# A tail reordered, its last product split, and each pair of row chunks stored by one transfer

## The chip, the cores and the metric

One core of a Trainium2 chip runs the kernel. The time is the device time of one execution in microseconds (us). The kernel before takes 466.84 us (median of 3 runs, 465.91 to 466.93). Kernels are compared only within the same rounds. Spans come from one profiled execution; its time is some 1.8 us longer than its span (before: 468.84 us for a span of 467.1).

Engines in the profile: PE is the matmul engine and PEld its weight loads, DVE is VectorE, ACT ScalarE, POOL GpSimd, SP SyncE. "SPq" is SyncE's sequencer while it issues a transfer. A transfer has landed when the last increment of its semaphore has come. A bank is a PSUM tile of 128x512 float32.

## The reference, cut to what matters

Two layers: attention with an exponential feature map, then a mix of the 64 lowest frequencies, a channel product and a rectifier.

```python
x = attention(q, k, v, w_phi)            # (8, 576, 512)
X = np.fft.rfft(x, axis=1)               # 64 modes are kept
Yr = Xr @ w_r - Xi @ w_i                 # one 512x512 product per mode
Yi = Xr @ w_i + Xi @ w_r
y = np.fft.irfft(Y, n=576, axis=1)
u = x + y
return u + np.maximum(u @ w_ch, 0.0)     # (8, 576, 512) float32, 9.44 MB
```

## The kernel before

The 64 modes are worked in eight "octets". The mode weights stream from DRAM until shortly before the end; the octet that needs the last of them is the last one. What this case is about comes after it: turn the last octet's sum (`yst`) and its product with `w_ch` (`zst`) back into rows, add them to the rows kept so far, rectify, and store 9.44 MB.

The rows of one pair of batches (`bp`) are cut into nine chunks of 128 rows. A row of a batch is `9 * p + c`, with `p` from 0 to 63. Chunk `n < 8` belongs to batch `n // 4`; on its partition `64 * a + p` it holds row `9 * p + 4 * a + n % 4`. Chunk 8 holds row `9 * p + 8` of both batches.

```python
pst_cm = tc.tile_pool(name="pst", bufs=8, space=bass.MemoryType.PSUM)   # eight single banks
...
    def back(p, c, bp, table, src, r, stop=True):          # frequencies back to rows
        if c < 8:
            pe.matmul(p, lhsT=table[r, c % 4, :], rhs=src[r, 2 * bp + c // 4, :], ...)
...
    class Absorb:           # octets 0 to 5 of one chunk, added into the kept rows
        def sums(self): ...                                # 3 matmuls into two banks
        def keep_x(self): ...                              # DVE: x += p
        def keep_w(self): ...                              # ACT: xw = q
...
    while mixq:             # one weight block after another
        mix(*key, wts.pop(key), XTb[g % 2], bank)
        ...
        if g == NG - 1 and i == 1:
            yst = pb.tile([128, DMODEL], BF16, name="yst")
            dve.tensor_tensor(out=yst, in0=py, in1=yacc[:, o, :], op=ALU.add)
            put(yst, o, yall, (0, 2))
            ...                                            # 4 transposes into pt
            act.copy(yT, pt)
            ...                                            # product: 4 matmuls of 512 columns
            act.copy(zst, pz)
            put(zst, o, zall, (1, 3))
...
    class Last:             # octets 6 and 7 and the store, two chunks at a time
        def base(self, which): ...                         # kept rows, by an identity
        def late(self, which): ...                         # octets 6, 7 from yl
        def straight(self, which): ...                     # octet 7 from yst, zst (first chunks)
        def relu(self): ...                                # ACT: rl = relu(q)
        def store(self):
            ...
            dve.tensor_tensor(out=o, in0=self.pp, in1=self.rl, op=ALU.add)   # 128x1024
            i, c = n // 4, n % 4
            for a in range(2):
                (sp, pool)[a].dma_start(
                    rows[i][:, 4 * a + c:4 * a + c + 2, :], o[64 * a:64 * a + 64])
```

A pair of chunks is thus stored by two transfers, one from SyncE and one from GpSimd. Each takes 64 partitions to 64 places of 4096 bytes.

Of the kernel before, what the change touches and what calls it, by code (L numbers as in the profile page):

```python
# [10 lines left out]
F32 = mybir.dt.float32  # L11
# [32 lines left out]
def kernel(  # L44
# [495 lines left out]
    pin_cm.__exit__(None, None, None)  # L540
    ps1_cm.__exit__(None, None, None)
    ps2_cm.__exit__(None, None, None)
    pst_cm = tc.tile_pool(name="pst", bufs=8, space=bass.MemoryType.PSUM)
    pst = pst_cm.__enter__()

    def bank(shape=(128, DMODEL), dt=F32):
        return pst.tile(list(shape), dt, name="pt", tag="pt")

    pb_cm = tc.tile_pool(name="pb", bufs=2)
    pb = pb_cm.__enter__()  # L550
# [3 lines left out]
    yl = pw.tile([128, B_, DMODEL], BF16, name="yl", tag="wt")  # L554
    CI = pb.tile([128, 5, 128], BF16, name="CI", bufs=1)
    CL = pb.tile([128, 5, 128], BF16, name="CL", bufs=1)
    CM = pb.tile([128, 4, 128], BF16, name="CM", bufs=1)


    def inverse_tables():  # L560
# [22 lines left out]
        def calc(in0, s1, s2, op0=ALU.mult, op1=ALU.add):  # L583
            f = small[:, used[1]:used[1] + 1]
            used[1] += 1
            dve.tensor_scalar(out=f, in0=in0, scalar1=s1, scalar2=s2, op0=op0, op1=op1)
            return f
# [4 lines left out]
        late = calc(calc(bits(pi, 4, 1), 8.0, 48.0), 1.0, jt)  # L592
        jm, tm, rm, b0 = bits(pi, 5, 3), bits(pi, 4, 1), bits(pi, 3, 1), bits(pi, 0, 7)
        last = calc(calc(tm, 4.0, jm), 1.0, 56.0)
        b0 = calc(b0, 0.0, 1.0, ALU.is_equal, ALU.mult)
        for dst, m, r, only in ((CI, mode, r, None), (CL, late, r, None), (CM, last, rm, b0)):
            n = 512 if only is not None else 640
            ph = calc(r, -S_ / 4.0, S_ / 4.0)
            amp = calc(r, -4.0 / S_, 2.0 / S_)
            if m is mode:  # L600
                half = calc(calc(m, 0.0, -0.5, ALU.is_equal, ALU.mult), 1.0, 1.0)
                amp = calc(amp, half, 0.0)
            if only is not None:
                amp = calc(amp, only, 0.0)
            dve.tensor_scalar(out=ang[:, :n], in0=tok[:, :n], scalar1=m, scalar2=ph,
                              op0=ALU.mult, op1=ALU.add)
            dve.tensor_scalar(out=rnd[:, :n], in0=ang[:, :n], scalar1=1.0 / S_, scalar2=MAGIC,
                              op0=ALU.mult, op1=ALU.add)
            dve.tensor_scalar(out=rnd[:, :n], in0=rnd[:, :n], scalar1=-MAGIC,
                              scalar2=-float(S_), op0=ALU.add, op1=ALU.mult)  # L610
            dve.tensor_tensor(out=ang[:, :n], in0=ang[:, :n], in1=rnd[:, :n], op=ALU.add)
            act.activation(rnd[:, :n], ang[:, :n], ACT.Sin, scale=2.0 * math.pi / S_)
            dve.tensor_scalar_mul(out=dst.rearrange("p c s -> p (c s)"), in0=rnd[:, :n],
                                  scalar1=amp)
# [31 lines left out]
    class Absorb:  # L646
# [3 lines left out]

        def sums(self):
            r = slice(0, 96)
            self.p, self.q = bank(), bank()
            back(self.p, self.n, self.bp, CI, yall, r)
            pe.matmul(self.q, lhsT=ident_b, rhs=xw[:, self.bp, self.n, :],
                      start=True, stop=False)
            back(self.q, self.n, self.bp, CI, zall, r)
# [25 lines left out]

        todo.append(both)
    ab = [Absorb(*c) for c in chunks]
    todo += [c.all for c in ab[:-3]]

    def fill(n):
        for _ in range(n):
            if todo:  # L690
                todo.pop(0)()

    def put(src, o, dst, copies):
        if o < 6:
            sp.dma_start(dst[16 * o:16 * o + 16], src)
        else:
            for s in copies:
                r = 32 * s + 16 * (o - 6)
                sp.dma_start(yl[r:r + 16], src)

    todo = [inverse_tables] + todo
    while mixq:
        key = mixq.pop(0)
        g, o, i = key[0], key[1] // 2, key[1] % 2
        if key not in wts:
            next_w(1)
        mix(*key, wts.pop(key), XTb[g % 2], bank)
        next_w(1)
        left = len(mixq)
        n = -(-max(len(todo) - 33, 0) // (left - 7)) if left > 7 else -(-len(todo) // max(left, 1))  # L710
        if g == NG - 1 and i == 1:
            py = pys.pop(o)
            yst = pb.tile([128, DMODEL], BF16, name="yst")
            dve.tensor_tensor(out=yst, in0=py, in1=yacc[:, o, :], op=ALU.add)
            put(yst, o, yall, (0, 2))
            end = left == 0
            if end:
                ab[-3].sums()
                ab[-3].keep_x()
            fill(min(n, 1))  # L720
            pt = bank([128, 4, 128], BF16)
            for dc in range(4):
                pe.transpose(pt[:, dc, :], yst[:, dc * 128:(dc + 1) * 128], ident_b)
            yT = pb.tile([128, 4, 128], BF16, name="yT")
            act.copy(yT, pt)
            if end:
                ab[-2].sums()
                ab[-2].keep_x()
                ab[-3].keep_w()
            fill(min(n - 1, 1))  # L730
            pz = bank()
            for dc in range(4):
                pe.matmul(
                    pz, lhsT=yT[:, dc, :], rhs=wchb[:, dc, :],
                    start=(dc == 0), stop=(dc == 3))
            zst = pb.tile([128, DMODEL], BF16, name="zst")
            act.copy(zst, pz)
            put(zst, o, zall, (1, 3))
            if end:
                ab[-2].keep_w()  # L740
                ab[-1].all()
            fill(max(n - 2, 0))
        else:
            fill(n)
    assert not todo
    pst_cm.__exit__(None, None, None)
    pst1 = ctx.enter_context(tc.tile_pool(name="pst1", bufs=4, space=bass.MemoryType.PSUM))
    pst2 = ctx.enter_context(tc.tile_pool(name="pst2", bufs=2, space=bass.MemoryType.PSUM))

    class Last:  # L750

        def __init__(self, bp, ns):
            self.bp, self.ns = bp, ns
            self.early = bp == 0 and ns[0] < 4

        def base(self, which):
            if which:
                self.q = [pst1.tile([128, DMODEL], F32, name="qq", tag="qq") for _ in self.ns]
            else:
                self.pp = pst2.tile([128, 2, DMODEL], F32, name="pp", tag="pp")  # L760
                self.p = [self.pp[:, a] for a in range(len(self.ns))]
            for a, n in enumerate(self.ns):
                if which:
                    pe.matmul(self.q[a], lhsT=ident_b, rhs=xw[:, self.bp, n, :],
                              start=True, stop=False)
                else:
                    pe.matmul(self.p[a].rearrange("p (g e) -> p g e", g=4), lhsT=ident_b,
                              rhs=chunk(self.bp, n), start=True, stop=False)
# [7 lines left out]
        def straight(self, which):  # L776
            if self.early:
                for a, n in enumerate(self.ns):
                    pe.matmul((self.q if which else self.p)[a], lhsT=CM[:, n],
                              rhs=(yst, zst)[which], start=False, stop=True)  # L780

        def relu(self):
            self.rl = pb.tile([128, 2, DMODEL], F32, name="rl")
# [1 line left out]
                act.activation(self.rl[:, a], self.q[a], ACT.Relu)  # L785

        def store(self):
            bp, n = self.bp, self.ns[0]
            rows = [out[2 * bp + i].rearrange("(p c) e -> p c e", c=9) for i in range(2)]
            if n == 8:  # L790
                o = pw.tile([128, DMODEL], F32, name="ofr", tag="wt")
                dve.tensor_tensor(out=o, in0=self.pp[:, 0], in1=self.rl[:, 0], op=ALU.add)
                for i in range(2):
                    (sp, pool)[i].dma_start(rows[i][:, 8, :], o[64 * i:64 * i + 64, :])
                return
            o = pw.tile([128, 2, DMODEL], F32, name="of", tag="wt")
            dve.tensor_tensor(out=o, in0=self.pp, in1=self.rl, op=ALU.add)
            i, c = n // 4, n % 4
            for a in range(2):
                (sp, pool)[a].dma_start(  # L800
                    rows[i][:, 4 * a + c:4 * a + c + 2, :], o[64 * a:64 * a + 64])

    seq = [Last(bp, ns) for bp in range(NP) for ns in ((0, 1), (2, 3), (4, 5), (6, 7), (8,))]
    seq[0].base(1)
    seq[0].late(1)
    seq[0].straight(1)
    seq[0].relu()
    for g, s in enumerate(seq):
        t = seq[g + 1] if g + 1 < len(seq) else None
        if t:  # L810
            t.base(1)
        s.base(0)
        if t:
            t.late(1)
        s.late(0)
        s.straight(0)
        if t:
            t.straight(1)
            t.relu()
        s.store()  # L820
# [31 lines left out]
```

## Time and profile before

| | before |
|---|---|
| time, median | 466.84 us |
| span of the profiled run | 467.1 us |
| last weights used by the last octet | 422.94 us |
| first store issued | 432.79 us |
| last addition ends | 458.2 us |
| DMA share while storing | 0.93 to 0.98 |

The first view is the table of busy time by stretch. Its columns are the stretch, its length, the busy time and instruction count of PE, PEld, DVE, ACT and POOL, the granted clock, the mean busy share of the 16 DMA engines, and the GB/s that they moved.

```profile
428.00:434.00 6.00, 5.74 (x31) 2.10 (x31) 1.53 (x2) 3.29 (x7) 0.55 (x1) 1.00 0.20 48
434.00:440.00 6.00, 6.00 (x37) 1.74 (x34) 4.98 (x5) 3.99 (x8) 2.12 (x4) 1.00 0.93 274
440.00:452.00 12.00, 12.00 (x72) 3.67 (x68) 10.26 (x10) 8.70 (x17) 4.75 (x9) 1.00 0.95 309
452.00:464.00 12.00, 5.03 (x30) 1.46 (x30) 5.50 (x5) 3.97 (x8) 3.19 (x6) 0.79 0.98 323
464.00:467.00 3.00, 0.00 (x0) 0.00 (x0) 0.00 (x0) 0.00 (x0) 0.00 (x0) 0.50 0.27 78
```

From 428 to 434 us the DMA engines are nearly idle. After that they are busy nearly all the time, at 274 and then at about 310 GB/s, and from 452 us on the compute engines run out of work first. The head of the tail therefore decides when the stores can start, and the stores decide how long it then takes.

The timeline of the head, in order of start (start, duration, engine, operation, output and inputs; in brackets the engine's idle time before it and what ended it):

```profile
422.94 0.67 PE L37 MATMUL pt<-wt,XT 128*32 128x512 bf16 x8 [1.67 <-DMA wt<-in_moe_w_i_dram]
...
423.65 0.69 DVE L37 TENSOR_TENSOR yst<-pt,yacc 128x512 bf16<-128x512 f32 x1 [2.09 <-PE pt L37]
...
424.89 0.58 ACT L37 COPY yT<-pt 128x512 bf16<-128x512 bf16 x1 [2.95 <-PE pt L37]
...
425.53 1.04 PE L37 MATMUL pt<-wchb,yT 128*128 128x512 bf16 x4
...
426.65 0.58 ACT L37 CAST zst<-pt 128x512 bf16<-128x512 f32 x1 [0.68 <-ACT xw L37]
...
431.53 1.23 DVE L37 TENSOR_TENSOR of<-pp,rl 128x1024 f32<-128x1024 f32 x1 [3.90 <-PE pp L37]
...
432.79 2.66 SPq L37 DMA_DIRECT2D out_dram<-of  x2
```

From the last octet's matmuls to the first store there are 9.85 us, nearly all of it serial.

### The profile page before, as it was taken

How to read it: one execution, taken by the hardware profiler on the slowest of the kernel's cores; microseconds unless marked ns; L12 is line 12 of the kernel's file. 1: busy time of each engine (PE TensorE's matmuls, PEld its weight loads, DVE VectorE, ACT ScalarE, POOL GpSimd, SP SyncE). 2: the span in 40 equal slices, each digit the busy share in tenths (PEclk: the TensorE clock that was granted, in tenths of full speed). 3: DMA queues.
4: the chain of work that ended last, by engine and by line, in shares of the span. 5: the costliest groups of instructions: out<-in, count | busy, mean ns of one | idle time of the engine just before them, and what ended most of it. 6: DMA issues, size and time to landing. Idle time of an engine off the chain costs nothing.

```text
span 467.1 us, 9757 instructions
## 1 busy us (share of the span) xinstructions
PE 337.8 (72%) x4084; PEld 207.5 (44%) x4084; DVE 269.1 (58%) x488; ACT 281.1 (60%) x475; POOL 92.7 (20%) x130
## 2 busy tenths in 40 slices
PE   0377677758788777788768778129997656997991
PEld 0246465636565555466546546005443322332330
DVE  5275877564666566777675676563331113773882
ACT  2566988766787786688777765123443323664771
POOL 5130322104112121122210112203221110000331
PEclk9998999888888798799997989659998997999996
DMA  8999999999999999999999999999999999992797
GB/s 193 207 177 220 226 210 228 229 229 136 225 208 229 229 213 222 229 209 227 229 229 207 229 207 208 207 207 207 207 214 214 216 216 211 207 177 50 241 317 254
DMA packets 86301, 99.27 MB, mean 213 GB/s; under 512 B 2800, under 2 KB 79728, under 8 KB 86256
## 3 DMA queue, kind: packets, MB, share of 16 engines
q0 software_dynamic: 77264, 81.80, 102.9%
q1 hardware_dynamic: 8992, 16.85, 11.8%
q8 instruction: 32, 0.52, 0.4%
q14 instruction: 13, 0.11, 0.1%
HBM read 163.64 MB, written 9.44 MB: 371 GB/s over the span
## 4 chain that ended last, share of the span: by engine, by line
issue 37%; DMA 21%; PE 16%; ACT 8%; POOL 8%; DVE 7%; POOLq 0%; ACTq 0%
PE pt L37 8%; DMA wt<-in_moe_w_r_dram 8%; DMA wt<-in_moe_w_i_dram 6%; DMA kb<-in_k_dram 5%; PE one L37 4%; POOL wt L37 4%; PE two L37 4%; DVE m L37 4%; ACT AQ L37 3%; DMA qb<-in_q_dram 3%; POOL out_dram L37 2%; ACT AB L37 2%; DVE zall L37 2%; ACT qT L37 1%; ACT kT L37 1%
## 5 line engine op out<-in xcount | busy, mean ns | idle before, releaser
L37 ACT CAST xw<-pt 128x512 bf16<-128x512 f32 x72 | 42.0, 586 | 59.5 <-PE pt L37 58.3
L37 ACT ACTIVATE AB<-two 128x1024 bf16<-128x1024 f32 x64 | 62.8, 1051 | 7.5 <-DVE mk L37 5.1
L37 ACT ACTIVATE AQ<-two 128x1024 bf16<-128x1024 f32 x64 | 63.1, 1055 | 2.8 <-PE two L37 2.6
L37 PE MATMUL pt<-wchb,xT 128*128 128x512 bf16 x144 | 38.6, 393 | 19.3 <-DVE xT L37 19.3
L37 DVE TENSOR_REDUCE m<-two 128x8 f32<-128x1024 f32 x32 | 39.2, 1224 | 19.4 <-PE two L37 19.3
L37 DVE TENSOR_REDUCE mk<-two 128x8 f32<-128x1024 f32 x32 | 38.9, 1219 | 19.5 <-PE two L37 19.0
L37 POOL DMA_DIRECT2D wt<-in_moe_w_i_dram x30 | 26.5, 882 | 110.1 <-PE one L37 63.8
L37 POOL DMA_DIRECT2D wt<-in_moe_w_r_dram x29 | 25.6, 881 | 95.7 <-PE one L37 62.0
L37 DVE TENSOR_TENSOR va<-vn,ee 128x1152 bf16<-128x1152 f32 x32 | 42.0, 1356 | 0.0
L37 DVE RECIPROCAL rd<-one 128x6 f32<-128x6 f32 x48 | 9.4, 196 | 50.3 <-PE one L37 50.3
L37 ACT COPY kT<-one 128x512 bf16<-128x512 bf16 (+1 forms) x32 | 19.2, 640 | 30.0 <-PE one L37 30.0
L37 PEld LDWEIGHTS <-minus 96*128 96x128 bf16 x288 | 27.4, 114 | 20.1 <-issue 14.8
L37 DVE TENSOR_TENSOR xs<-pt,xs 128x512 bf16<-128x512 f32 x36 | 24.3, 691 | 18.9 <-PE pt L37 18.5
L37 PE MATMUL two<-qT,w2blk 128*128 128x512 bf16 x64 | 29.9, 467 | 6.3 <-ACT AQ L37 6.3
L37 PEld LDWEIGHTS <-XT 128*32 128x32 bf16 x512 | 18.0, 179 | 35.9 <-issue 22.9
L37 PE MATMUL two<-w2blk,qT 128*128 128x256 bf16 x128 | 21.2, 292 | 16.5 <-ACT AB L37 11.9
L37 DVE COPY xT<-pt 128x512 bf16<-128x512 bf16 x36 | 15.1, 422 | 27.9 <-PE pt L37 27.9
L37 PEld LDWEIGHTS <-xs 128*128 128x128 bf16 x304 | 24.1, 98 | 14.9 <-issue 7.6
L37 PE MATMUL two<-mT,minus 96*128 96x128 bf16 x256 | 30.3, 252 | 0.0
L37 PE MATMUL pt<-wt,XT 128*32 128x512 bf16 x208 | 18.6, 434 | 13.6 <-DMA wt<-in_moe_w_i_dram 9.9
L37 PEld LDWEIGHTS <-qT 128*128 128x128 bf16 x144 | 14.4, 103 | 31.3 <-issue 28.4
L37 DVE TENSOR_TENSOR xs<-one,rd 128x384 bf16<-128x384 f32 x48 | 26.8, 558 | 1.6
(113 smaller groups left out, 679.3 us busy)
## 6 DMA issues: line engine op xcount, KB each, us to landing
wt<-in_moe_w_i_dram POOLq DMA_DIRECT2D x30, 1024.0 KB, 23.7
wt<-in_moe_w_r_dram POOLq DMA_DIRECT2D x29, 1024.0 KB, 23.9
vn<-in_v_dram SPq DMA_DIRECT2D x16, 576.0 KB, 7.8
kb<-in_k_dram POOLq DMA_DIRECT2D x16, 288.0 KB, 17.6
qb<-in_q_dram POOLq DMA_DIRECT2D x16, 288.0 KB, 17.7
out_dram<-of SPq DMA_DIRECT2D x16, 256.0 KB, 5.8
out_dram<-of POOLq DMA_DIRECT2D x16, 256.0 KB, 5.3
yacc<-in_moe_w_r_dram POOLq DMA_DIRECT2D x1, 1024.0 KB, 12.5
```

The costliest lines, as they stand in the source:

```text
L37: ins = f(*args, **kwargs)
```

## The change

Its intent is to start the stores earlier and to issue fewer of them. The first two chunks are handled one by one and in PSUM banks of their own; all that doesn't depend on the last octet is summed before it. The last product runs in halves of 256 columns, with ACT and DVE each copying one half. All 36 chunks are absorbed before the last octet (before: 33). And every pair is stored by one transfer of 128 partitions, by SyncE and GpSimd in turn. The ninth chunk, in before two stores of 64 rows, becomes one store of 128 rows from SyncE, with 128 in front on its DRAM side; that is not in the cut.

```diff
-    pst_cm = tc.tile_pool(name="pst", bufs=8, space=bass.MemoryType.PSUM)
+    pst = ctx.enter_context(tc.tile_pool(name="pst", bufs=4, space=bass.MemoryType.PSUM))
+    pst2 = ctx.enter_context(tc.tile_pool(name="pst2", bufs=2, space=bass.MemoryType.PSUM))
...
-    todo += [c.all for c in ab[:-3]]
+    todo += [c.all for c in ab]
...
+        if not mixq:                                  # just ahead of the last octet
+            for l in seq[:2]:
+                for which in (1, 0):
+                    l.base(which)
+                    l.late(which)
         mix(*key, wts.pop(key), XTb[g % 2], bank)
...
+            for h in range(2):                        # yst, yT, product and zst in halves
+                dve.tensor_tensor(out=yst[:, H * h:H * h + H], ...)
...
+            act.copy(zst[:, 0:H], pz[0])
+            dve.tensor_copy(zst[:, H:], pz[1])
...
         def store(self):
-            i, c = n // 4, n % 4
-            for a in range(2):
-                (sp, pool)[a].dma_start(
-                    rows[i][:, 4 * a + c:4 * a + c + 2, :], o[64 * a:64 * a + 64])
+            eng = (sp, pool)[n // 2 % 2]
+            rows = out[2 * bp + n // 4]
+            eng.dma_start(
+                bass.AP(tensor=rows.tensor, offset=rows.offset + n % 4 * DMODEL,
+                        ap=[[4 * DMODEL, 2], [9 * DMODEL, 64], [1, w * DMODEL]]),
+                o.rearrange("p a e -> p (a e)") if w > 1 else o)
...
-    seq = [Last(bp, ns) for bp in range(NP) for ns in ((0, 1), (2, 3), (4, 5), (6, 7), (8,))]
+    seq[0:1] = [Last(0, (0,)), Last(0, (1,))]
```

The partitions are `64 * a + p`, so the DRAM side of one transfer has to count `a` (2) first, then `p` (64), then the row.

More of the change, by code (lines that the diff above doesn't have):

```diff
@@ L542, with banks @@
     ps2_cm.__exit__(None, None, None)
-    pst_cm = tc.tile_pool(name="pst", bufs=8, space=bass.MemoryType.PSUM)
-    pst = pst_cm.__enter__()
+    pst = ctx.enter_context(tc.tile_pool(name="pst", bufs=4, space=bass.MemoryType.PSUM))
+    pst2 = ctx.enter_context(tc.tile_pool(name="pst2", bufs=2, space=bass.MemoryType.PSUM))
     def bank(shape=(128, DMODEL), dt=F32):
         return pst.tile(list(shape), dt, name="pt", tag="pt")
+    def banks(dt=F32):
+        return pst2.tile([128, 2, DMODEL * (1 if dt == F32 else 2)], dt, name="pp", tag="pp")
     pb_cm = tc.tile_pool(name="pb", bufs=2)
@@ L556 @@
     CL = pb.tile([128, 5, 128], BF16, name="CL", bufs=1)
-    CM = pb.tile([128, 4, 128], BF16, name="CM", bufs=1)
+    CM = CF.rearrange("p c r m -> p (c r m)")[:, 0:1024].rearrange(
+        "p (i c s) -> p i c s", i=2, c=4)
     def inverse_tables():
@@ L594, in inverse_tables @@
         last = calc(calc(tm, 4.0, jm), 1.0, 56.0)
-        b0 = calc(b0, 0.0, 1.0, ALU.is_equal, ALU.mult)
-        for dst, m, r, only in ((CI, mode, r, None), (CL, late, r, None), (CM, last, rm, b0)):
+        b0, b1 = (calc(b0, float(i), 1.0, ALU.is_equal, ALU.mult) for i in range(2))
+        for dst, m, r, only in ((CI, mode, r, None), (CL, late, r, None), (CM[:, 0], last, rm, b0),
+                                (CM[:, 1], last, rm, b1)):
             n = 512 if only is not None else 640
@@ L652, in sums @@
             r = slice(0, 96)
-            self.p, self.q = bank(), bank()
+            if chunks.index((self.bp, self.n)) % 2:
+                self.p, self.q = bank(), bank()
+            else:
+                t = banks()
+                self.p, self.q = t[:, 0], t[:, 1]
             back(self.p, self.n, self.bp, CI, yall, r)
@@ L698, in put @@
                 r = 32 * s + 16 * (o - 6)
-                sp.dma_start(yl[r:r + 16], src)
+                (sp, pool)[s // 2 if o == 7 else 0].dma_start(yl[r:r + 16], src)
     todo = [inverse_tables] + todo
-    while mixq:
-        key = mixq.pop(0)
-        g, o, i = key[0], key[1] // 2, key[1] % 2
-        if key not in wts:
-            next_w(1)
-        mix(*key, wts.pop(key), XTb[g % 2], bank)
-        next_w(1)
-        left = len(mixq)
-        n = -(-max(len(todo) - 33, 0) // (left - 7)) if left > 7 else -(-len(todo) // max(left, 1))
-        if g == NG - 1 and i == 1:
-            py = pys.pop(o)
-            yst = pb.tile([128, DMODEL], BF16, name="yst")
-            dve.tensor_tensor(out=yst, in0=py, in1=yacc[:, o, :], op=ALU.add)
-            put(yst, o, yall, (0, 2))
-            end = left == 0
-            if end:
-                ab[-3].sums()
-                ab[-3].keep_x()
-            fill(min(n, 1))
-            pt = bank([128, 4, 128], BF16)
-            for dc in range(4):
-                pe.transpose(pt[:, dc, :], yst[:, dc * 128:(dc + 1) * 128], ident_b)
-            yT = pb.tile([128, 4, 128], BF16, name="yT")
-            act.copy(yT, pt)
-            if end:
-                ab[-2].sums()
-                ab[-2].keep_x()
-                ab[-3].keep_w()
-            fill(min(n - 1, 1))
-            pz = bank()
-            for dc in range(4):
-                pe.matmul(
-                    pz, lhsT=yT[:, dc, :], rhs=wchb[:, dc, :],
-                    start=(dc == 0), stop=(dc == 3))
-            zst = pb.tile([128, DMODEL], BF16, name="zst")
-            act.copy(zst, pz)
-            put(zst, o, zall, (1, 3))
-            if end:
-                ab[-2].keep_w()
-                ab[-1].all()
-            fill(max(n - 2, 0))
-        else:
-            fill(n)
-    assert not todo
-    pst_cm.__exit__(None, None, None)
-    pst1 = ctx.enter_context(tc.tile_pool(name="pst1", bufs=4, space=bass.MemoryType.PSUM))
-    pst2 = ctx.enter_context(tc.tile_pool(name="pst2", bufs=2, space=bass.MemoryType.PSUM))
     class Last:
@@ L753, in __init__ @@
             self.bp, self.ns = bp, ns
-            self.early = bp == 0 and ns[0] < 4
+            self.early = bp == 0 and ns[0] < 6
+            self.first = bp == 0 and ns[0] < 2
         def base(self, which):
-            if which:
-                self.q = [pst1.tile([128, DMODEL], F32, name="qq", tag="qq") for _ in self.ns]
+            if self.first:
+                if which:
+                    self.pp = banks()
+                    self.q, self.p = [self.pp[:, 1]], [self.pp[:, 0]]
+            elif which:
+                self.q = [bank() for _ in self.ns]
             else:
-                self.pp = pst2.tile([128, 2, DMODEL], F32, name="pp", tag="pp")
+                self.pp = banks()
                 self.p = [self.pp[:, a] for a in range(len(self.ns))]
@@ L778, in straight, with keep_p @@
                 for a, n in enumerate(self.ns):
-                    pe.matmul((self.q if which else self.p)[a], lhsT=CM[:, n],
+                    pe.matmul((self.q if which else self.p)[a], lhsT=CM[:, n // 4, n % 4],
                               rhs=(yst, zst)[which], start=False, stop=True)
+        def keep_p(self):
+            self.rl = pb.tile([128, 2, DMODEL], F32, name="rl")
+            act.copy(self.rl[:, 0], self.p[0])
         def relu(self):
@@ L787, in store @@
         def store(self):
-            bp, n = self.bp, self.ns[0]
-            rows = [out[2 * bp + i].rearrange("(p c) e -> p c e", c=9) for i in range(2)]
+            bp, n, w = self.bp, self.ns[0], len(self.ns)
+            eng = (sp, pool)[n // 2 % 2]
+            if w == 1:
+                o = pw.tile([128, DMODEL], F32, name="ofr", tag="wt")
+            else:
+                o = pw.tile([128, 2, DMODEL], F32, name="of", tag="wt")
+            if n == 0 and self.first:
+                dve.scalar_tensor_tensor(out=o, in0=self.q[0], scalar=0.0, in1=self.rl[:, 0],
+                                         op0=ALU.max, op1=ALU.add)
+            elif w == 1:
+                dve.tensor_tensor(out=o, in0=self.p[0], in1=self.rl[:, 0], op=ALU.add)
+            else:
+                dve.tensor_tensor(out=o, in0=self.pp, in1=self.rl, op=ALU.add)
@@ L790, in store @@
             if n == 8:
-                o = pw.tile([128, DMODEL], F32, name="ofr", tag="wt")
-                dve.tensor_tensor(out=o, in0=self.pp[:, 0], in1=self.rl[:, 0], op=ALU.add)
-                for i in range(2):
-                    (sp, pool)[i].dma_start(rows[i][:, 8, :], o[64 * i:64 * i + 64, :])
+                eng.dma_start(
+                    out[2 * bp:2 * bp + 2].rearrange("i (p c) e -> (i p) c e", c=9)[:, 8, :], o)
                 return
-            o = pw.tile([128, 2, DMODEL], F32, name="of", tag="wt")
@@ L797, in store @@
-            dve.tensor_tensor(out=o, in0=self.pp, in1=self.rl, op=ALU.add)
-            i, c = n // 4, n % 4
-            for a in range(2):
-                (sp, pool)[a].dma_start(
-                    rows[i][:, 4 * a + c:4 * a + c + 2, :], o[64 * a:64 * a + 64])
-    seq = [Last(bp, ns) for bp in range(NP) for ns in ((0, 1), (2, 3), (4, 5), (6, 7), (8,))]
-    seq[0].base(1)
-    seq[0].late(1)
-    seq[0].straight(1)
-    seq[0].relu()
+            rows = out[2 * bp + n // 4]
+            eng.dma_start(
+                bass.AP(tensor=rows.tensor, offset=rows.offset + n % 4 * DMODEL,
+                        ap=[[4 * DMODEL, 2], [9 * DMODEL, 64], [1, w * DMODEL]]),
+                o.rearrange("p a e -> p (a e)") if w > 1 else o)
@@ new lines @@
+    seq = [Last(bp, ns) for bp in range(NP) for ns in ((0, 1), (2, 3), (4, 5), (6, 7), (8,))]
+    seq[0:1] = [Last(0, (0,)), Last(0, (1,))]
+    H = DMODEL // 2
+    while mixq:
+        key = mixq.pop(0)
+        g, o, i = key[0], key[1] // 2, key[1] % 2
+        if key not in wts:
+            next_w(1)
+        if not mixq:
+            assert not todo
+            for l in seq[:2]:
+                for which in (1, 0):
+                    l.base(which)
+                    l.late(which)
+        mix(*key, wts.pop(key), XTb[g % 2], bank)
+        next_w(1)
+        left = len(mixq)
+        n = -(-max(len(todo) - 36, 0) // (left - 7)) if left > 7 else -(-len(todo) // max(left, 1))
+        if g == NG - 1 and i == 1:
+            end = left == 0
+            py = pys.pop(o)
+            yst = pb.tile([128, DMODEL], BF16, name="yst")
+            pt = [bank([128, 2, 128], BF16) for h in range(2)]
+            yT = [pb.tile([128, 2, 128], BF16, name=f"yT{h}") for h in range(2)]
+            for h in range(2):
+                dve.tensor_tensor(out=yst[:, H * h:H * h + H], in0=py[:, H * h:H * h + H],
+                                  in1=yacc[:, o, H * h:H * h + H], op=ALU.add)
+            put(yst, o, yall, (0, 2))
+            if not end:
+                fill(min(n, 1))
+            for h in range(2):
+                for dc in range(2):
+                    pe.transpose(pt[h][:, dc, :],
+                                 yst[:, H * h + 128 * dc:H * h + 128 * dc + 128], ident_b)
+                if h:
+                    dve.tensor_copy(yT[h], pt[h])
+                else:
+                    act.copy(yT[h], pt[h])
+            if not end:
+                fill(min(n - 1, 1))
+            else:
+                for l in seq[:2]:
+                    l.straight(0)
+                seq[0].keep_p()
+            pz = [bank([128, H]) for e in range(2)]
+            for h in range(2):
+                for e in range(2):
+                    for dc in range(2):
+                        pe.matmul(
+                            pz[e], lhsT=yT[h][:, dc, :],
+                            rhs=wchb[:, 2 * h + dc, H * e:H * e + H],
+                            start=(h == dc == 0), stop=(h == dc == 1))
+            zst = pb.tile([128, DMODEL], BF16, name="zst")
+            act.copy(zst[:, 0:H], pz[0])
+            dve.tensor_copy(zst[:, H:], pz[1])
+            put(zst, o, zall, (1, 3))
+            fill(max(n - 2, 0))
+        else:
+            fill(n)
@@ L808 @@
+    assert not todo
+    for l in seq[:2]:
+        l.straight(1)
+    seq[1].relu()
     for g, s in enumerate(seq):
-        t = seq[g + 1] if g + 1 < len(seq) else None
+        t = seq[g + 1] if 0 < g < len(seq) - 1 else None
         if t:
             t.base(1)
-        s.base(0)
+        if g > 1:
+            s.base(0)
         if t:
             t.late(1)
-        s.late(0)
-        s.straight(0)
+        if g > 1:
+            s.late(0)
+            s.straight(0)
         if t:
```

## The prediction

> **What bounds the kernel now.** Until about 423 us the weights' stream: the busy table by stretch has a DMA share of 1.2 at 205 to 229 GB/s; the timeline shows the matmuls of the last octet starting at 422.94 us, after 1.67 us of idle ended by the last weights' DMA. Then comes a serial head: sum of the last octet (DVE 0.69 us), transposes, copy (ACT 0.58), product (PE 1.04), copy (ACT 0.58), the first chunks' sums, the first 128x1024 addition at 431.53 us, the first store issued at 432.79. From 434 us the stores are bound by the DMA: in stretches of 2 us its share is 0.9 to 1.0 at 290 to 334 GB/s until 464 us, though the last addition ends at 458.2. End: 467.1.
>
> **What the change does.** (1) Head: the first two chunks are summed before the last octet, the last product runs in halves on ACT and DVE, and 128x512 stores go first. From these durations: first store about 4.4 us after the last octet's matmuls start, instead of 9.85. Against that, three more absorbed chunks (0.65 us of PE each in the timeline) and eight matmuls of 0.22 us now precede the last octet: 3.7 us, where PE idled 0.73 + 1.67 us before the last two octet passes. The octet slips by about 1.3 us; net gain of the head about 4 us. (2) Another inverse table, 256-wide pieces in earlier octets, fewer single banks: under the weights, near zero.
>
> (3) Stores: one transfer per pair, written to DRAM as [2][64][row], slowest dimension 2. The replaced ones had 64 rows there. [...] In the packet records a 4096-byte store takes 159 ns (median), a 2048-byte one 84. [...] 7 pairs x 64 x 159 ns = 71 us, two first chunks x 64 x 84 ns = 11 us, the 128-row chunks 3 us[...]: about 95 us, an estimate, in series. From 429 us that ends at 524, plus about 2 us to completion.
>
> **Critical path.** The head's 4 us are on it; the stores then take about 97 us in place of 34.
>
> **Prediction: 525 us, range 495 to 555.** Faster by over 2%: 0.02; within 2%: 0.12; slower by over 2%: 0.86.
>
> **What would show each step.** Right: first store issued near 428.5 us; SyncE's pairs land 10 us or more after issue (now 5.8), queueing; GB/s falls from some 320 to below 120 after about 433 us, with DMA share below 0.4, and to about 50 at the end; DVE's additions wait for buffers held by stores; the time to the last octet is unchanged within 2 us.
>
> **What would make it wrong.** If one transfer still spreads over all 16 engines, the stores stay bound at some 320 GB/s and only the head counts: about 463 us. [...] If two engines alone exceed 26 GB/s each, because packets overlap, it is under 510.

What the sum under (3) needs was the assumption that a transfer with a 2 in front on its DRAM side runs on two engines, and all of SyncE's on the same two, so that their packets follow in series. The sum came to about 95 us: the three terms that stand make 85, and a term of 10 us for one of GpSimd's eight pairs is cut. For the "about 2 us to completion", before's last packet ends at 465.5 us and its span at 467.1. The "26 GB/s" are 4096 bytes in 159 ns, 25.8.

## More of the kernel before

The view of everything that writes the output gives one line per engine and tile (count; shortest, median and longest issue in ns; first and last start), and the time from issue to landing:

```profile
L37 SPq DMA_DIRECT2D out_dram<-of x16: 466/798/1817, 432.8 to 459.8; - x16
L37 POOL DMA_DIRECT2D out_dram<-of x16: 523/526/545, 433.1 to 457.9; - x16
...
DMA to landing us min/median/max: 3.1/5.5/6.9
```

## The result, and the profile after

The changed kernel takes 538.27 us (median of 4 runs, 537.23 to 542.16), the kernel before 466.88 us beside it. The ratio is 1.154 with a 95% interval of 1.148 to 1.161. A ratio in this document is the mean time of one kernel's fast runs over the mean of the other's in the same rounds, so it is not quite the ratio of the medians quoted.

The same table by stretch, for the changed kernel:

```profile
428.00:434.00 6.00, 5.50 (x30) 2.05 (x32) 2.90 (x4) 3.16 (x7) 0.95 (x2) 1.00 0.35 83
434.00:440.00 6.00, 6.00 (x34) 1.90 (x33) 4.62 (x5) 3.71 (x8) 1.19 (x2) 1.00 0.26 56
440.00:452.00 12.00, 2.74 (x16) 0.72 (x14) 1.49 (x2) 1.83 (x4) 0.79 (x1) 0.71 0.43 118
452.00:464.00 12.00, 5.18 (x15) 1.00 (x15) 1.88 (x3) 1.68 (x3) 0.79 (x1) 0.50 0.34 110
...
520.00:537.00 17.00, 0.00 (x0) 0.00 (x0) 0.00 (x0) 0.00 (x0) 0.00 (x0) 0.50 0.10 39
```

Everything is idle at once: the DMA share is a third, and PE, DVE and ACT work a few of twelve microseconds. An average over 16 engines can hide a few that are always busy.

The timeline of the head:

```profile
424.63 0.69 PE L37 MATMUL pt<-wt,XT 128*32 128x512 bf16 x8
425.37 0.76 DVE L37 TENSOR_TENSOR yst<-pt,yacc 128x256 bf16<-128x256 f32 x2 [2.90 <-PE pt L37]
...
426.17 0.37 ACT L37 COPY yT<-pt 128x256 bf16<-128x256 bf16 x1 [3.14 <-PE pt L37]
...
426.74 1.04 PE L37 MATMUL pt<-wchb,yT 128*128 128x256 bf16 x8
...
427.63 0.37 ACT L37 CAST zst<-pt 128x256 bf16<-128x256 f32 x1 [0.33 <-PE pt L37]
...
428.77 0.69 DVE L37 SCALAR_TENSOR_TENSOR ofr<-pp,rl 128x512 f32<-128x512 f32 x1 [0.48 <-PE pp L37]
...
429.49 1.38 SPq L37 DMA_DIRECT2D out_dram<-ofr  x2
...
432.06 1.23 DVE L37 TENSOR_TENSOR of<-pp,rl 128x1024 f32<-128x1024 f32 x1 [1.75 <-PE pp L37]
```

The last octet starts 1.69 us later than before (424.63 against 422.94), although the last weights' packet is no later (422.1 against 422.5 us in the packet records). The first store is issued 4.86 us after the octet's start in place of 9.85, so 3.3 us earlier in all. The first full pair, however, is added no sooner than before (432.06 against 431.53; it is the second pair of rows, whose addition starts at 433.69 in before).

The transfers to the output, and then two lines of the list of waits after 420 us (engine and line, what it waited for, us in total, times, longest):

```profile
L37 POOL DMA_DIRECT2D out_dram<-of x8: 787/787/808, 433.6 to 503.8; - x8
L37 SPq DMA_DIRECT2D out_dram<-of x7: 512/1296/8923, 435.5 to 502.4; - x7
L37 SPq DMA_DIRECT2D out_dram<-ofr x6: 534/5184/9251, 429.5 to 512.2; - x6
...
DMA to landing us min/median/max: 21.9/30.5/36.0
```

```profile
DVE ofr L37 <- DMA out_dram<-of: 23.1, 3, 8.0
DVE of L37 <- DMA out_dram<-of: 22.4, 3, 10.0
```

A transfer lands 30.5 us after its issue (5.5 before), DVE waits for stores to give back its buffers, and SyncE itself is held for up to 9.25 us while it issues (1.9 in before; 0.6 in e9_perm, below).

The records of the semaphores tell more. In before each store leaves 16 increments of its semaphore there. Here SyncE's seven pairs leave three each, of which two come late (us; the pair's issue, then its last two increments):

```
issue    435.5   447.5   452.6   473.9   478.4   497.4   502.4
last-1   463.3   474.3   485.4   497.2   507.5   520.2   530.4
last     463.8   477.0   487.3   501.0   511.3   524.4   534.6
```

They follow each other by 10.2 to 13.7 us, one after the other.

GpSimd's pairs land late too. The one issued at 441.5 us has ten increments by 447.0, four between 456.6 and 461.8, and its last two at 474.8 and 477.5, each 0.5 us after the last two of SyncE's pair of 447.5. GpSimd's next pair ends in the same way (485.7 and 487.6, against 485.4 and 487.3). So these transfers, and the buffers that they hold, seem to be kept to the pace of SyncE's pairs; the records don't name the engine, and what holds them back is not shown.

### The profile page after: what moved, and what is told of

It is laid out like the page before. It is cut to its first block, busy times and chain, and to the rows that moved or that the text cites. A ratio compares the mean times of both kernels' runs of the same rounds, so it can differ in the third digit from the quotient of the medians.

```text
span 536.6 us, 9795 instructions
## 1 busy us (share of the span) xinstructions
PE 342.4 (64%) x4075; PEld 210.6 (39%) x4120; DVE 277.1 (52%) x522; ACT 276.9 (52%) x476; POOL 89.5 (17%) x120
## 4 chain that ended last, share of the span: by engine, by line
DMA 32%; issue 19%; PE 19%; ACT 14%; DVE 9%; POOL 3%; POOLq 0%; DVEq 0%; ACTq 0%; SPq 0%
DMA out_dram<-of 13%; DMA wt<-in_moe_w_i_dram 10%; DMA qb<-in_q_dram 8%; PE one L37 7%; PE two L37 5%; DVE m L37 5%; ACT AQ L37 5%; ACT AB L37 5%; PE pt L37 4%; PE pp L37 3%; DVE mk L37 2%; POOL wt L37 2%; ACT kT L37 2%; ACT qT L37 1%; DMA zall<-zst 1%
## 5 line engine op out<-in xcount | busy, mean ns | idle before, releaser
L37 ACT ACTIVATE AQ<-two 128x1024 bf16<-128x1024 f32 x64 | 63.1, 1057 | 2.7 <-PE two L37 2.6
L37 PE MATMUL pt<-wchb,xT 128*128 128x512 bf16 x135 | 39.8, 410 | 25.6 <-DVE xT L37 24.3
L37 ACT CAST xw<-pt 128x512 bf16<-128x512 f32 x54 | 31.7, 588 | 45.2 <-PE pt L37 45.0
L37 ACT ACTIVATE rl<-pt 128x512 f32<-128x512 f32 x34 | 18.6, 595 | 54.9 <-DVE of L37 33.8
L37 PE MATMUL pp<-xs,ident_b 128*128 128x512 bf16 x36 | 14.7, 484 | 37.7 <-DVE of L37 27.6
L37 DVE TENSOR_TENSOR of<-pp,rl 128x1024 f32<-128x1024 f32 x15 | 18.2, 1224 | 37.8 <-DMA out_dram<-of 22.4
L37 PEld LDWEIGHTS <-minus 96*128 96x128 bf16 x288 | 26.2, 109 | 19.5 <-issue 13.8
L37 PE MATMUL two<-mT,minus 96*128 96x128 bf16 x256 | 29.1, 245 | 3.1 <-issue 1.8
L37 PEld LDWEIGHTS <-xT 128*128 128x128 bf16 x144 | 13.6, 104 | 35.5 <-DVE xT L37 24.1
```

Of the source, the lines that this page charges most:

```text
L37: ins = f(*args, **kwargs)
```

## The experiments

Theory A, from the prediction: the transfer with a 2 in front on its DRAM side runs on two DMA engines. That was an assumption; no trace had shown it. Rival B: one 512 KB transfer per pair is too large or too few (buffers are held longer, less is in flight). Rival C: the new order, the fewer single banks and the split product cost the time. Theory D came after the first run and is stated there.

| run | head | store of a pair | median us | ratio to before, 95% interval |
|---|---|---|---|---|
| before | old | two of 64 rows | 468.2 to 469.1 | 1 |
| after | new | one, 2 in front | 538.27 | 1.154 [1.148, 1.161] |
| e2_pairs | old | one, 2 in front | 536.63 | 1.147 [1.142, 1.152] |
| e1_halves | new | two of 64 rows | 469.13 | 1.002 [0.999, 1.005] |
| e7_even | new | two of 64 rows, ninth chunk too | 468.26 | 1.000 [0.996, 1.004] |
| e10_before_perm | old | one, 64 in front | 465.93 | 0.995 [0.991, 0.999] |
| e9_perm | new | one, 64 in front | 464.14 | 0.993 [0.988, 0.998] |
| e11_later | new, four matmuls moved | one, 64 in front | 463.68 | 0.991 [0.986, 0.995] |
| e3_rows | new, strided writes early | one, 64 in front | 473.27 | 1.012 [1.008, 1.016] |
| e5_rows | new, strided reads early | one, 64 in front | 476.22 | 1.019 [1.014, 1.025] |
| e6_before_rows | old, strided reads early | one, 64 in front | 477.64 | 1.020 [1.016, 1.024] |
| e8_pool | new | one, 2 in front, all from GpSimd | 515.34 | one run |

All outputs but those of e4_counts were correct. Three of the six of e5_rows (482.57 to 484.14 us) are left out of its row.

### e1_halves: only the stores undone

```diff
-            eng.dma_start(bass.AP(..., ap=[[4 * DMODEL, 2], [9 * DMODEL, 64], [1, w * DMODEL]]), ...)
+            for a in range(2):
+                (sp, pool)[a].dma_start(rows[:, 4 * a + c:4 * a + c + w, :], o[64 * a:64 * a + 64])
```

> The changed kernel with one thing undone: each pair, and each of the two first chunks, is again stored by two transfers of 64 rows, one from SyncE and one from GpSimd. Theory A (a store whose DRAM side starts with a dimension of 2 runs on two DMA engines): about 463 us, which is before less the 3.3 us by which the first store is issued earlier (429.5 against 432.8), pairs landing in some 5 to 6 us, DMA share of 0.9 or more from 434 us on. Rival B (one 512 KB transfer per pair is too large: fewer transfers in flight, buffers held too long): also about 463, so this run doesn't tell A from B. Rival C (the new order, the fewer single banks and the split product cost the time): stays above 520 us.

Measured: 469.13 us, 1.002 [0.999, 1.005] of before. C falls: with the new head, banks and products in place and the stores of the pairs as before, nothing is lost. (The ninth chunk keeps its one transfer here; e7_even splits it too.) But nothing is gained either, and the 463 us of A and B was off by 6 us in that: the stores did start earlier, at 429.25 us. Where the lead went can be read from the ends of the two kernels. First the last addition and SyncE's last issue of before, then those of e1_halves:

```profile
457.56 0.68 DVE L37 TENSOR_TENSOR ofr<-pp,rl 128x512 f32<-128x512 f32 x1
...
461.49 1.92 SPq L37 DMA_DIRECT2D out_dram<-ofr  x1
```

```profile
456.61 0.68 DVE L37 TENSOR_TENSOR ofr<-pp,rl 128x512 f32<-128x512 f32 x1
...
461.54 0.93 SPq L37 DMA_DIRECT2D out_dram<-ofr  x1
```

Of the 3.3 to 3.5 us at the first store 0.95 us is left at the last addition. PE is busy throughout 430 to 454 us in both and hands over a pair at a time: the second pair is added 1.9 us ahead of before (433.04 against 434.9 us), the first pair of the next batches 1.0 us ahead (439.3 against 440.3). And that last microsecond is lost in the queue: SyncE issues its last store 3.2 us after the addition ended in before, 4.3 us in e1_halves, at the same time. From this comes theory D: the store stream, not its start, sets the end, because with halves the issue falls behind the additions.

### e2_pairs: only the stores changed

```diff
-            for a in range(2):
-                (sp, pool)[a].dma_start(rows[i][:, 4 * a + c:4 * a + c + 2, :], o[64 * a:64 * a + 64])
+            (sp, pool)[n // 2 % 2].dma_start(
+                bass.AP(..., ap=[[4 * DMODEL, 2], [9 * DMODEL, 64], [1, 2 * DMODEL]]), ...)
```

> The kernel before with one thing added: each pair is stored by one transfer with the 2 in front, from SyncE and GpSimd in turn; nothing of the head is changed. Theory A: SyncE has eight pairs of 64 packets on each of two engines at the 161 ns that the changed kernel's trace shows from packet to packet, 82 us[...], and some 8 us of gaps as in the changed kernel: from 433 us that ends near 534, time about 536 us. Rival B: as slow, some 535 to 545. Rival C: about 467 us.

A term of 10 us for one of GpSimd's pairs, which no trace shows, is cut from theory A's sum; with it the terms came to 100 us.

Measured: 536.63 us, 1.147 [1.142, 1.152]. This one statement carries the whole loss; A and B both said so to within a few us, C is out. The profiled spans of e2_pairs and of the changed kernel are both 536.6 us: here too the new head's earlier start leaves no trace. A possible reason is that the new head sends SyncE's first pair as two stores with packets of 2048 bytes: 128 of them at 109 ns in the mean are 14.0 us on each of theory A's two engines, 64 packets of 4096 bytes at 168 ns are 10.8. That is an estimate from the packet records, and not tested.

### e3_rows: one transfer per pair, with 64 in front

The transfers stay as large, as few and on the same queues. Only the order of the rows on the partitions changes: partition `2 * p + a` in place of `64 * a + p`, so the DRAM side counts 64 first.

```diff
-    ap=[[4 * DMODEL, 2], [9 * DMODEL, 64], [1, w * DMODEL]]
+    ap=[[9 * DMODEL, 64], [4 * DMODEL, 2], [1, w * DMODEL]]
...                                   # the exponentials of q, written in the new order
-    o = t[:, ab].rearrange("f c j h a p -> f a c (j h) p")
+    o = t[:, ab].rearrange("f c j h p a -> f a c (j h) p")
...                                   # forward and inverse tables in the same order
```

> The changed kernel with one transfer per pair kept, 512 KB each and from the same queues, but the rows of a chunk are dealt to the partitions the other way round (partition 2p+a holds row p of half a), so that the DRAM side reads [64][2][row]: the 64 in front. Tables and the layout of the exponentials are permuted to match. Theory A: all 16 engines, pairs land in some 6 to 8 us, about 463 us (up to 466 if the writes of the exponentials with a stride cost something early). Rival B: the transfers are as large and as few as in the changed kernel, so it stays above 520. Rival C: stays above 520.

Measured: 473.27 us, 1.012 [1.008, 1.016]. B falls: 512 KB transfers that land in 3.6 us (median, 3.0 to 5.3) are no burden, and the loss of 70 us is gone. The 463 to 466 us expected were missed because the strided write cost more early than thought. These are the exponentials' lines of before and of e3_rows (shortest, median, longest in ns):

```profile
L37 ACT ACTIVATE AQ<-two x64: 1018/1057/1139, 31.0 to 284.9; 128x1024 bf16<-128x1024 f32 x64
```

```profile
L37 ACT ACTIVATE AQ<-two x64: 1300/1348/1454, 30.9 to 293.3; 128x1024 bf16<-128x1024 f32 x64
```

64 of them are 18.6 us more of ACT. The last weights' packet came at 428.7 us in place of 422.5. From there to the end of the span e3_rows takes 41.3 us, before 44.6.

### e4_counts: the transfers by themselves

A kernel that does nothing but store, one transfer at a time; its output is wrong.

```python
store(eng, [[gap * ROW, n], [ROW, 64 // n]], parts=64)      # 256 KB, n of 2, 4, 8, 16; three each
store(eng, [[4 * DMODEL, 2], [ROW, 64]], parts=128)         # a pair, 2 in front
store(eng, [[ROW, 64], [4 * DMODEL, 2]], parts=128)         # a pair, 64 in front
```

> Store times by themselves; the output is wrong on purpose. 256 KB stores of 64 packets of 4096 bytes, one at a time, from SyncE and then from GpSimd, with 2, 4, 8 and 16 in front (three each), then one 512 KB pair with 2 in front and one with 64 in front. Theory A: beyond a fixed part of about 2 us the landing takes 64 / n packets of 161 ns: 5.2, 2.6, 1.3 and 0.6 us for n of 2, 4, 8 and 16, 10.3 us for the pair with 2 in front and 1.3 us with 64 in front; the number of late increments of the semaphore is n for SyncE. Rival B: the time follows the bytes alone, the same for all 256 KB stores, and the same for both pairs.

Measured, from the records of issues, packets and semaphores (us from issue to the last increment; for n of 2 to 16 the first of three, the others within 0.8 us):

```
                         SyncE                       GpSimd
in front   bytes     landed  late increments     landed  late increments  4-byte packets
2          256 KB     9.08      2                  8.75      2               464
4          256 KB     5.50      4                  5.49      4               208
8          256 KB     3.64      8                  3.46      8                80
16         256 KB     2.87     16                  2.71     16                16
2 (pair)   512 KB    12.79      2                 13.66      2               912
64 (pair)  512 KB     3.02     16                  2.97     16                16
```

The same bytes in the same 4096-byte packets land in 12.79 us or in 3.02 us; B's "bytes alone" is refuted. For n of 2, 4, 8 and 16 in front the late increments are n, with 64 in front 16. From SyncE, with fewer than 16 late ones, a first increment comes 1 us after the issue, and then the n late ones. From GpSimd there are always 16, of which n are late. The DMA share fits theory A: it is 0.10 from 94 to 108 us, around SyncE's pair with 2 in front, and 0.32 from 109 to 113 us, around the one with 64. Of 16 engines that is 22 and 20 us of packets, so over the landing some 2 and 7 engines at work at a time, an estimate. The packets of 4 bytes come on top of the 64 or 128 of 4096 bytes; the changed kernel has 7296 of them on GpSimd's queue from 433 us on, 912 for each of its eight pairs. What they are for was not followed up.

With 16 in front, SyncE's landing less four packets of 161 ns leaves 2.2 us, where about 2 were expected as the fixed part. The size was a little off for n of 2 and 4: 7.2 and 4.6 us had been expected, because the packets of these stores took 210 to 216 ns in the mean with a median of 159. Why was not followed up.

### e5_rows and e6_before_rows: the same order, its early cost moved

The permuted order is now read by the matmul that feeds the exponentials; the exponentials are written straight. e5_rows has the new head, e6_before_rows the old one.

```diff
-    rhs=self.qT[:, 4 * i:4 * i + 4, :].rearrange("p n s -> p (n s)"),
+    rhs=self.qT[:, 4 * i:4 * i + 4, :].rearrange("p (a j) s -> p j s a", a=2),
```

> The run before with 64 in front again, without its early cost: there the exponentials were written with a stride (1348 ns in place of 1055, the last octet 7 us late at 431.9). Here the matmuls read the permuted order instead and the exponentials are written straight. Theory A with theory D (the store stream, not its start, sets the end: with 64-row halves SyncE's issue falls 3 us behind the additions, with 512 KB transfers over all engines it doesn't): the octet at about 424.5, the last addition at about 457.3 as in the halves' run, the end 5.2 us after it as in the first run with 64 in front: a span of 462.5, about 0.988 of before. Rival (the head alone gives nothing whatever the stores, since the engines behind it set the pace): no faster than the next run. If the matmuls' strided reads cost as much as the strided writes: about 470.

> The kernel before, its head untouched, with nothing but the pairs stored by one transfer each with 64 in front (same permuted reads as the run above). Theory D: the last addition at 458.2 as before, the end 5.2 us after it: 463.4, about 0.990 of before; the head's own worth is then the 1 us or so between this run and the one above. If the head is worth its 3.3 us of earlier first store, this run is 3 us slower than the one above. If one transfer per pair is not better than two halves: as before, 1.000.

Measured: 476.22 us (1.019; the median of the three fast runs, that of all six is 481.06) and 477.64 us (1.020). Both missed: this is the branch "if the strided reads cost as much", and they cost more. The matmul's line in before and in e5_rows:

```profile
L37 PE MATMUL two<-qT,w2blk x64: 375/382/635, 26.3 to 283.2; 128*128 128x512 bf16 x64
```

```profile
L37 PE MATMUL two<-qT,w2blk x64: 643/685/769, 26.2 to 296.1; 128*128 128x512 bf16 x64
```

The last weights came at 431.9 and 431.3 us. As totals these two runs say nothing about the tail. Counted from the last weights' packet, e5_rows takes 40.8 us and e6_before_rows 44.2.

### e7_even: the halves' run, its ninth chunk in halves too

```diff
-            if n == 8: eng.dma_start(out[2 * bp:2 * bp + 2].rearrange(...)[:, 8, :], o)
+            if n == 8:
+                for i in range(2): (sp, pool)[i].dma_start(..., o[64 * i:64 * i + 64, :])
```

> The halves' run with one more thing undone: the ninth chunk of each group of batches is stored in two halves from both queues, as before, so that SyncE has 1 MB and not 1.25 MB of each group. In the halves' run GpSimd's packets ended at 462 and SyncE went on alone at some 231 GB/s to 465.7. If that imbalance ate the head's lead: about 1 us less than the halves' run, 0.998 of before. If not: the same as the halves' run, 1.002.

Measured: 468.26 us, 1.000 [0.996, 1.004], against 1.002 [0.999, 1.005]. The intervals overlap, so whether the uneven queues cost anything is not resolved. What is clear is that the new head, with halves, gives nothing in either form.

### e8_pool: every transfer with a 2 in front from GpSimd

```diff
-            eng = (sp, pool)[n // 2 % 2]
+            eng = sp if n == 8 else pool
```

> The changed kernel, its transfers with the 2 in front kept, but all of them issued by GpSimd; SyncE keeps the four stores of 128 rows. [...] with six buffers in flight and 14 us each the additions end near 470, time 472 to 490 us. Rival A2 (GpSimd's transfers too always take the same two engines): 15 pairs of 10.3 us and two of 5.5 in series, over 590 us. Rival B (size and number of transfers): about 538, as the changed kernel.

472 to 490 us is theory A's.

Measured: 515.34 us, one run. A2 is out (over 590 was said for GpSimd's transfers on the same two engines). B's 538 is missed too. A's size was missed by 25 us. The 21 transfers to the output took 21.0 us to land in the median (6.2 to 28.1), GpSimd's 17 alone 22.2 us, not 14, and DVE's additions stood still up to 16 us at a time for their buffers (one ends at 446.9 us, the next starts at 463.0). What stretched them was not tested. The packet records don't name the engine, so how these transfers are dealt to the engines is not shown.

### e9_perm, e10_before_perm and e11_later: the order changed in the last stage alone

The kept rows enter the last stage through a matmul with an identity. A permuted identity gives them in another order with the same matmuls, and the two late tables get their columns permuted once. The early phase isn't touched.

```diff
+    dve.tensor_copy(perm_b.rearrange("k (p a) -> k a p", a=2),
+                    ident_f.rearrange("k (a p) -> k a p", a=2))
...
-    pe.matmul(self.q[a], lhsT=ident_b, rhs=xw[:, self.bp, n, :], ...)
+    pe.matmul(self.q[a], lhsT=perm_b if n < 8 else ident_b, rhs=xw[:, self.bp, n, :], ...)
...                                   # the same for self.p; CL and CM: tok permuted
-    ap=[[4 * DMODEL, 2], [9 * DMODEL, 64], [1, w * DMODEL]]
+    ap=[[9 * DMODEL, 64], [4 * DMODEL, 2], [1, w * DMODEL]]
```

e9_perm is the changed kernel with this, e10_before_perm the kernel before with this and one transfer per pair. e11_later is e9_perm ("the run before last" in its text) with the second chunk's four early matmuls placed after the last octet's.

> The changed kernel with the rows dealt to the partitions only in the last stage: a permuted identity as the stationary operand of the base sums, and permuted columns of the two late tables, so that the early phase isn't touched and each pair is one transfer with 64 in front. The two runs with 64 in front and a slowed early phase took 41.3 and 40.8 us from the last weights' packet to the end (before 44.6, the halves' runs 45.3 and 43.6). Theory D: the same 41 us from 422.2: a span of 463, 0.990 of before or a little less. If the gain of those runs came from their slower early phase and not from the transfers: 1.000.

> The kernel before, its old head, with the same late permutation and one transfer per pair with 64 in front: the fourth corner beside before, the even halves' run and the run above. Its slowed twin took 44.2 us from the last weights' packet to the end, so theory D (each of the two parts alone gives about nothing, the two together 3 to 4 us) says a span of 466.5, 0.998 of before. If the transfers alone carry the gain: about 463, 0.990.

> The run before last with one more step: the four matmuls of the second chunk come after the last octet's, in the time in which the tensor engine waits for the octet's sum, not ahead of it. In the changed kernel's trace these four took 1.3 us and the octet started 2.4 us after the last weights. If the head is on the critical path once the stores run on all engines: 0.5 to 1 us less than that run, 0.988 of before. If the additions' pace alone sets the end: no difference.

Measured: e9_perm 464.14 us, 0.993 [0.988, 0.998]; e10_before_perm 465.93 us, 0.995 [0.991, 0.999]; e11_later 463.68 us, 0.991 [0.986, 0.995]; before 469.06 us. All three beat the kernel before, by under one per cent. e9_perm came out as expected. e10_before_perm did better than the 0.998 expected: the transfers alone give the larger part, about 0.5%, and the head's 0.2% on top is within the intervals. e11_later gained 0.1 to 0.2% over e9_perm, which is not resolved either; its first store came no earlier (427.58 against 427.45 us), so it doesn't settle the question that it was built for.

Counted from the last weights' packet to the end of the profiled span, before takes 44.6 us, e10_before_perm 42.1, e9_perm 40.7 and e11_later 42.1. These are single executions, but the first three give the order of the medians: the transfers alone give some 2.5 us, and the head may give 1 or 2 more.

Why the stores are better is to be read in e9_perm's table by stretch, its list of transfers, and the end of e10_before_perm (last addition, SyncE's last issue):

```profile
434.00:440.00 6.00, 6.00 (x36) 1.84 (x35) 5.04 (x5) 4.44 (x9) 1.23 (x2) 1.00 0.84 330
440.00:452.00 12.00, 12.00 (x71) 3.69 (x69) 9.85 (x10) 8.74 (x16) 1.82 (x3) 1.00 0.90 352
```

```profile
L37 POOL DMA_DIRECT2D out_dram<-of x8: 608/608/622, 431.9 to 455.1; - x8
L37 SPq DMA_DIRECT2D out_dram<-of x7: 538/539/545, 433.4 to 453.5; - x7
...
DMA to landing us min/median/max: 3.0/3.5/5.1
```

```profile
457.76 0.68 DVE L37 TENSOR_TENSOR ofr<-pp,rl 128x512 f32<-128x512 f32 x1
...
458.46 0.50 SPq L37 DMA_DIRECT2D out_dram<-ofr  x1
```

352 GB/s in place of 309, a landing in 3.5 us in place of 5.5, and in e10_before_perm the last issue right behind the end of the last addition (458.46 against 458.44 us) in place of 3.2 us after it: with these stores the issue no longer falls behind, as theory D said. The head isn't needed for that: e10_before_perm moves 321, 348 and 378 GB/s from 440 to 452 us and lands in 3.9 us. In the packet records of the tail a 4096-byte packet took 202 to 203 ns in the mean in before, and 164 (SyncE) and 170 (GpSimd) in e10_before_perm; why was not followed up. The other half of theory D, as e10_before_perm's text put it (each part alone gives about nothing), was not borne out. That the additions' pace, and not the DMA, now sets the end fits PE, which is busy all along in both, but no run tested it. The profiled span of e9_perm (460.7 us) flatters it: in that execution the last weights came at 420.0 us, 2.5 us earlier than in before, so the medians are to be trusted.

## Why the prediction was right or wrong

**Two engines: right in number, which engines not shown.** The change of one access pattern costs 1.147 by itself (e2_pairs), the same transfers with 64 in front cost nothing (e3_rows, e9_perm), and alone on the chip the pair lands in 12.79 us against 3.02 (e4_counts) with two late increments. From 520 to 530 us in the changed kernel, where the last of SyncE's pairs are alone with data, the packet records hold 125 packets of 4096 bytes at 159 ns, 19.9 us of packets in 10 us: two engines' worth (DMA share 0.13; 51 GB/s, so not over 26 each). That SyncE's pairs all have the same two was not shown, only that they end one after the other, 10.2 to 13.7 us apart.

**The length of the two-engine stream: in series as said, the size 9% short.** The prediction's term was "about 95 us"; the stores' packets of 2048 bytes and more ran from 430.8 to 534.9 us, 104 us. The term that was mis-sized is "in the packet records a 4096-byte store takes 159 ns (median), a 2048-byte one 84": a sum of packets in series needs the mean. In the changed kernel SyncE's packets took 168 and 109 ns in the mean, and the 4096-byte ones of GpSimd's pairs 194. With these, SyncE's 448 x 168 + 160 x 109 ns are 93 us in place of 85, and the term for one of GpSimd's pairs, 64 x 194 ns, is 12 us in place of 10: 105 us, an estimate. This accounts for 10 of the 13 us between 525 and 538; the rest is the stream's start at 430.8 in place of 429 us and the 1.8 us by which a time is longer than its span. The term for one of GpSimd's pairs remains an assumption: it fits this sum, but no record names the engine, and a late last increment doesn't show it, since all of GpSimd's pairs have one (21.9 to 36.0 us).

**The head: right in its durations, wrong in "the head's 4 us are on it".** The octet slipped by 1.69 us (1.3 predicted), the first store came 4.86 us after it (4.4 predicted), so 3.3 us were gained at the first store. They were not gained at the end: 1.002 and 1.000 with halves, and no gain of the changed kernel over e2_pairs. What was left out, as e1_halves shows, is that the following pairs wait for PE, which is busy all along, so the lead melts to about 1 us within one group of batches, and that SyncE's issue then lags anyway.

**"Under the weights, near zero": nothing speaks against it.** With the new banks, tables and halves in place the last weights' packet came no later (422.1 against 422.5 us) and e1_halves is at 1.002; no run takes this part by itself.

**The signs in the profile.** First store near 428.5: 429.49. Landing of 10 us or more: 21.9 to 36.0. Below 120 GB/s after 433 us: 56, 118, 110. DMA share below 0.4: 0.26, 0.43, 0.34, so once above. About 50 GB/s at the end: 51 between 520 and 530 us. DVE waiting for buffers: yes.

**The branch not taken.** "If one transfer still spreads over all 16 engines ... about 463 us" is e9_perm, which is 0.993 of before, or 463.6 us on 466.88 us. The number fits by luck, its reason ("only the head counts") doesn't: the transfers carry most of it, and the stores did not stay at 320 GB/s (352).

## What to carry to other kernels

When two transfers are merged into one, look at the slowest dimension of its DRAM side as the instruction carries it: with a 2 in front of 64 rows a pair landed in 12.79 us here, with two late increments, and the kernel lost 15%; with 64 in front the same bytes landed in 3.02 us and gained half a per cent (0.1 to 0.9). If the order of the rows is in the way, a permuted identity in a matmul that is there anyway changed it here without a loss (0.995 and 0.993), whereas strided writes (1348 ns in place of 1057) or reads (685 in place of 382) in a busy phase delayed the last weights by 6 to 9 us. An earlier first store was worth nothing measurable here where the work behind it could not keep up, so follow the lead to the end before counting it.
